# Transposing V and wq inside their own buffers in the backward part of a decode block

## The chip, the cores and the metric

The kernel runs on one core of one Trainium2 chip. The metric is device time in microseconds (us), the median over executions; the profile's span is one execution without its launch edges. A ratio is the mean time of one kernel's fast runs over that of the other's fast runs of the same rounds on the same chip, so it is not quite the ratio of the medians beside it.

## The reference

The reference is a pre-LayerNorm decode block and its gradients: attention of 4 x 32 heads over a cache of 4096 rows of 128, then a SwiGLU layer. It returns the output and the gradients of x, K, V and all weights. What matters for the change is the backward part of a head. With P the softmax row, dO the gradient of the head's output and c their constant:

```python
dV[k, :] = P[k] * dO                      # 1 MB per head, written
dP[k]    = V[k, :] . dO                   # needs V again, contracted over its 128 columns
dS[k]    = P[k] * (dP[k] - c) * scale
dK[k, :] = dS[k] * q                      # 1 MB per head, written
dx       = dq @ wq.T                      # needs wq transposed
```

K and V are read in the forward part, V is read a second time in the backward part, and dK and dV are written: 5 x 128 MB, nearly all of the traffic.

## The kernel before

Large tiles live in 23 slots of 8320 bytes per partition, handed out from a first-in first-out list `free`. A slot taken again waits for whatever its last user still does, for a gradient until its write has landed.

```python
class Slot:
    def __init__(self, name, src=free):
        self.i = src.popleft()
        self.t = slotp.tile([P, SLOT], BF16, name=name, tag=f"slot{self.i}")
    ...
    def give(self):
        free.append(self.i)
```

In the backward part V comes into 6 slots of a ring of its own (`vring`), is transposed on TensorE in blocks of 8 through PSUM, and ScalarE copies the blocks to a second slot, VT. That frees V's slot; VT is freed after the dP matmuls.

```python
def V_T(s, ps, part=range(SJ // GW)):
    if s not in VTs:
        VTs[s] = Slot("VT")
    VT, Vn = VTs[s].heads(), V2s[s].heads()
    for g in part:
        pt = ps.tile([P, GW, P], BF16, tag="tps", name="pt_tps")      # 2 PSUM buffers in the loop
        for i in range(GW):
            nc.tensor.transpose(pt[:, i, :], Vn[:, g * GW + i, :], ident_b[:])
        nc.scalar.copy(out=VT[:, g * GW:(g + 1) * GW, :], in_=pt[:])
    ...
    sl = V2s.pop(s)
    (vring if len(V2s) + len(vring) < NV2 else free).append(sl.i)

def front(s):
    ...
    for j in range(SJ):
        nc.tensor.matmul(dP_ps[:, j:j + 1], lhsT=VT[:, j, :], rhs=dOT_bf[:, s:s + 1], start=True, stop=True)
    VTs.pop(s).give()

for s in range(NH):                       # cut: the side work of the weight gradients
    prefetch()                            # loads V into every slot in vring
    front(s + 1); grad_V(s + 1); grad_K(s)
```

`grad_V` and `grad_K` each take a slot, fill it with one VectorE product, and have POOL issue its write to HBM.

## Time and profile before

| | before |
|---|---|
| median time of the first 3 runs | 1725.89 us |
| bytes moved | 707.88 MB |
| DMA share from 740 to 1700 us | 1.01 |
| busiest engine, PE | 77% of the span |

The prediction below shows the lines on the DMA. The other side of the picture is who waits for whom from 740 to 1700 us, the backward loop. The columns are the waiting engine, its line, what it waited for, us in total, times, longest.

```profile
POOL out_dram L780 <- DVE dSt L1162: 248.6, 86, 10.4
...
DVE gv L769 <- DMA out_dram<-gk: 128.5, 36, 11.7
PE pt_tps L759 <- ACT VT L760: 123.8, 131, 10.0
...
POOL out_dram L1169 <- DMA out_dram<-gk: 64.0, 21, 5.0
...
ACT VT L760 <- DMA out_dram<-gk: 53.8, 16, 8.5
```

The last line is what the change is aimed at. ScalarE (ACT) wants to copy a transposed block to VT, but the slot it was handed is still being written out as a K gradient. PE then waits for ScalarE (third line), and POOL for VectorE, which waits for dP (first line). The second line is a wait of the same kind by VectorE for its own output slot.

### The profile page before, as it was taken

The page shows a single profiled execution, that of the slowest core. Times are in us where ns is not written, and L with a number is a line of the kernel's source. Part 1 is how long each engine was busy: PE and PEld are TensorE (multiplying, and loading weights), DVE is VectorE, ACT ScalarE, POOL GpSimd, SP SyncE. Part 2 cuts the span into 40 slices and gives each one's busy share as a digit, 9 for nine tenths or more (in the row PEclk, how much of TensorE's full clock was granted, in tenths as well). Part 3 has the DMA queues.
Part 4 walks back from the last instruction along what each step waited for, and adds up shares of the span by engine and source line. Part 5 has one row for each costly group of instructions (what it writes and reads, how often), then busy time and mean ns, then how long its engine had stood idle before and what let it go on. Part 6 is the DMA issues. An engine that isn't in the chain of part 4 may idle for free.

```text
span 1721.7 us, 44266 instructions
## 1 busy us (share of the span) xinstructions
PE 1330.3 (77%) x19124; PEld 1129.6 (66%) x19124; DVE 1253.5 (73%) x1389; ACT 960.7 (56%) x1470; POOL 422.6 (25%) x808
## 2 busy tenths in 40 slices
PE   5889888888888888877688787786778677877672
PEld 4677666676666666867577677675666555656562
DVE  5989899989998997666766666665575566556573
ACT  3455444544444444667555555555666667766662
POOL 1211232222222231211322222221122223122231
PEclk9999999999999999666655555555675566555555
DMA  9999999999999999999999999999999999999997
GB/s 398 418 419 418 419 418 419 418 413 419 417 417 405 419 403 390 373 419 420 418 415 411 416 410 410 412 417 419 423 417 413 419 417 414 418 416 414 414 417 314
DMA packets 101868, 707.88 MB, mean 411 GB/s; under 512 B 11284, under 2 KB 15392, under 8 KB 17704
## 3 DMA queue, kind: packets, MB, share of 16 engines
q1 hardware_dynamic: 62272, 422.60, 59.5%
q0 software_dynamic: 39008, 282.37, 40.1%
q8 instruction: 150, 2.46, 0.5%
q14 instruction: 46, 0.38, 0.1%
q10 hardware_dynamic: 392, 0.07, 0.0%
HBM read 422.59 MB, written 282.34 MB: 409 GB/s over the span
## 4 chain that ended last, share of the span: by engine, by line
DMA 47%; DVE 6%; PE 4%; issue 3%; ACT 2%; POOL 0%; POOLq 0%; DVEq 0%; ACTq 0%
DMA out_dram<-gk 29%; DMA out_dram<-gv 14%; DVE gk L769 3%; DVE gv L769 2%; DMA out_dram<-gwq 2%; DMA out_dram<-gw 2%; ACT VT L760 1%; PE pt_tps L759 1%; PE M_ps L433 1%; DVE PK L418 1%; PE pt_w L562 0%; PE pt_wo L571 0%; ACT Pn L397 0%; POOL P L1143 0%; PE kP_ps L443 0%
## 5 line engine op out<-in xcount | busy, mean ns | idle before, releaser
L760 ACT COPY VT<-pt_tps 128x1024 bf16<-128x1024 bf16 x512 | 493.0, 1016 | 248.7 <-PE pt_tps L759 140.5
L759 PE MATMUL pt_tps<-ident_b,V 128*128 128x128 bf16 x4096 | 455.2, 293 | 129.6 <-ACT VT L760 125.2
L759 PEld LDWEIGHTS <-V 128*128 128x128 bf16 x4096 | 403.6, 138 | 193.3 <-issue 182.9
L769 DVE TENSOR_TENSOR gv<-P,reps 128x4096 bf16<-128x4096 bf16 x125 | 286.5, 2292 | 233.9 <-DMA out_dram<-gk 131.2
L769 DVE TENSOR_TENSOR gk<-dS,reps 128x4096 bf16<-128x4096 bf16 x128 | 293.4, 2292 | 99.7 <-DMA out_dram<-gv 55.8
L433 PE MATMUL M_ps<-PK,Vn 128*128 128x130 bf16 x4096 | 284.6, 222 | 49.0 <-DMA Vn<-in_A_v_cache_dram 48.6
L418 DVE TENSOR_TENSOR PK<-Kn,PK 128x4096 bf16<-128x4096 bf16 x128 | 292.3, 2283 | 31.6 <-POOL PK L414 31.2
L433 PEld LDWEIGHTS <-Vn 128*128 128x128 bf16 x4096 | 251.4, 99 | 70.3 <-DMA Vn<-in_A_v_cache_dram 64.2
L325 DVE STREAM_TRANSPOSE KT<-Kn 128x512 f32<-128x512 f32 (+1 forms) x321 | 250.6, 797 | 0.3 <-issue 0.2
L320 ACT COPY KT<-pt_tps 128x1024 bf16<-128x1024 bf16 x128 | 129.4, 1012 | 191.5 <-PE pt_tps L319 148.8
L1153 PE MATMUL dP_ps<-dOT_bf,VT 128*128 128x1 bf16 x4096 | 152.5, 166 | 66.3 <-ACT VT L760 65.0
L1153 PEld LDWEIGHTS <-VT 128*128 128x128 bf16 x4096 | 141.1, 104 | 78.5 <-ACT VT L760 77.4
L1169 POOL DMA_DIRECT2D out_dram<-gk x128 | 68.0, 531 | 374.0 <-DVE gk L769 250.4
L780 POOL DMA_DIRECT2D out_dram<-gv x128 | 68.2, 533 | 328.9 <-DVE dSt L1162 258.8
L331 POOL TENSOR_TENSOR W<-qrep,wmask 128x128 bf16<-128x128 bf16 x128 | 123.2, 963 | 83.4 <-PE S_ps L351 68.5
L414 POOL COPY PK<-P_all 128x64 bf16<-128x64 bf16 x128 | 32.4, 253 | 420.9 <-ACT P_all L408 417.9
L1143 POOL COPY P<-P_all 128x64 bf16<-128x64 bf16 x125 | 103.6, 829 | 0.0
L408 ACT COPY P_all<-pt_P 32x64 bf16<-32x64 bf16 x256 | 51.9, 203 | 58.9 <-PE pt_P L404 56.7
L319 PE MATMUL pt_tps<-ident_b,Kn 128*128 128x128 bf16 x1024 | 80.5, 223 | 0.0
L443 PE MATMUL kP_ps<-PK,onesw 128*32 128x512 bf16 x1024 | 79.6, 388 | 0.0
L319 PEld LDWEIGHTS <-Kn 128*128 128x128 bf16 x1024 | 62.0, 100 | 25.9 <-issue 25.8
L397 ACT ACTIVATE Pn<-E,rl 128x1024 bf16<-128x1024 f32 x64 | 73.7, 1152 | 3.3 <-DVE rl L394 3.2
(237 smaller groups left out, 1315.3 us busy)
## 6 DMA issues: line engine op xcount, KB each, us to landing
Kn<-in_A_k_cache_dram SPq DMA_DIRECT2D x128, 1024.0 KB, 15.4
Vn<-in_A_v_cache_dram SPq DMA_DIRECT2D x128, 1024.0 KB, 16.0
V<-in_A_v_cache_dram SPq DMA_DIRECT2D x128, 1024.0 KB, 10.7
out_dram<-gv POOLq DMA_DIRECT2D x128, 1024.0 KB, 24.8
out_dram<-gk POOLq DMA_DIRECT2D x128, 1024.0 KB, 25.3
wq<-in_A_wq_dram SPq DMA_DIRECT2D x8, 1024.0 KB, 13.2
out_dram<-gw POOLq DMA_DIRECT2D x6, 896.0 KB, 26.8
wo<-in_A_wo_dram SPq DMA_DIRECT2D x4, 1024.0 KB, 13.3
```

The lines of the kernel that those rows point to most:

```text
L319: nc.tensor.transpose(pt[:, i, :], Kn[:, c * GW + i, :], ident_b[:])
L320: nc.scalar.copy(out=KT[:, c * GW:(c + 1) * GW, :], in_=pt[:])
L325: nc.vector.transpose(out=KT[:, c * w_:(c + n) * w_], in_=Kn[:, c * w_:(c + n) * w_])
L331: nc.gpsimd.tensor_tensor(out=W[:, hl], in0=qrep[:, :, s:s + 1].to_broadcast([P, 4, 32]), in1=wmask[:, hl, None, :].to_broadcast([P, 4, 32 ...
L418: nc.vector.tensor_tensor(out=PK[:, :, 0:Dh].rearrange("p j (r t) -> p j r t", t=2), in0=Ks[s].heads().rearrange("p j (r t) -> p j r t", t=2),
L433: nc.tensor.matmul(hold["M"][:], lhsT=Vn[:, j, :], rhs=PK[:, j, :], start=(j == 0), stop=(j == SJ - 1))
L443: nc.tensor.matmul(hold["kP"][32 * q:32 * (q + 1), :, :], lhsT=ones_window(w), rhs=PK[:, j0:j0 + 4, 0:Dh], start=(w == 0 and c == 0), stop ...
L759: nc.tensor.transpose(pt[:, i, :], Vn[:, g * GW + i, :], ident_b[:])
L760: nc.scalar.copy(out=VT[:, g * GW:(g + 1) * GW, :], in_=pt[:])
L769: nc.vector.tensor_tensor(out=dst.rearrange("p j (r t) -> p j r t", t=2), in0=col2[:, :, None, :].to_broadcast([P, SJ, Dh // 2, 2]), in1=r ...
L1143: nc.gpsimd.tensor_copy(out=P2s[s][:], in_=P_all[:, s, :, None].to_broadcast([P, SJ, 2]))
L1153: nc.tensor.matmul(dP_ps[:, j:j + 1], lhsT=VT[:, j, :], rhs=dOT_bf[:, s:s + 1], start=True, stop=True)
```

## The change

The transposes write back into the block that they came from, so VT needs no slot. V's ring grows from 6 to 7 slots, and one more V is read ahead before the loop starts. wq in the dx stage is treated in the same way. The arithmetic and the order of the instructions stay, except for these slots and one V load.

```diff
     def V_T(s, ps, part=range(SJ // GW)):
         if s not in VTs:
-            VTs[s] = Slot("VT")
-        VT, Vn = VTs[s].heads(), V2s[s].heads()
+            VTs[s] = V2s.pop(s)
+        v = VTs[s].heads()
         for g in part:
 ...
-                nc.tensor.transpose(pt[:, i, :], Vn[:, g * GW + i, :], ident_b[:])
-            nc.scalar.copy(out=VT[:, g * GW:(g + 1) * GW, :], in_=pt[:])
-        if part[-1] < SJ // GW - 1:
-            return
-        sl = V2s.pop(s)
-        (vring if len(V2s) + len(vring) < NV2 else free).append(sl.i)
+                nc.tensor.transpose(pt[:, i, :], v[:, g * GW + i, :], ident_b[:])
+            nc.scalar.copy(out=v[:, g * GW:(g + 1) * GW, :], in_=pt[:])
 ...
-    NV2 = 6
+    NV2 = 7
 ...
-        while len(free) > 2:
+        while len(free) > 1:
             load_V2()
 ...
-            wqT = Slot("wqT")
 ...
-                    nc.scalar.copy(out=wqTv[:, h0:h0 + 8, :], in_=pt[:])
-                wq2.give()
+                    nc.scalar.copy(out=wv[:, h0:h0 + 8, :], in_=pt[:])
 ...
-            VTs.pop(s).give()
+            sl = VTs.pop(s)
+            (vring if len(V2s) + len(VTs) + len(vring) < NV2 else free).append(sl.i)
 ...
-                    V_T(1, psT)
                     first_gv[0].give()
```

More of the change, by code (lines that the diff above doesn't have):

```diff
@@ L985, in side_work @@
                 yield
-            wqTv = wqT.b(HD).rearrange("p (n c) -> p n c", c=P)
             for cc in range(DC):
@@ L992, in side_work @@
                 wq2 = wq2s.popleft()
+                wv = wq2.b(HD).rearrange("p (n c) -> p n c", c=P)
                 for h0 in range(0, H, 8):
@@ L995, in side_work @@
                     for i in range(8):
-                        nc.tensor.transpose(pt[:, i, :], wq2.b(HD)[:, (h0 + i) * P:(h0 + i + 1) * P], ident_b[:])
+                        nc.tensor.transpose(pt[:, i, :], wv[:, h0 + i, :], ident_b[:])
                     yield
-                    nc.scalar.copy(out=wqTv[:, h0:h0 + 8, :], in_=pt[:])
-                wq2.give()
+                    nc.scalar.copy(out=wv[:, h0:h0 + 8, :], in_=pt[:])
                 yield
                 for h in range(H):
-                    nc.tensor.matmul(dx_ps[0:B, cc * P:(cc + 1) * P], lhsT=dqT_bf[:, h * B:(h + 1) * B], rhs=wqTv[:, h, :],
+                    nc.tensor.matmul(dx_ps[0:B, cc * P:(cc + 1) * P], lhsT=dqT_bf[:, h * B:(h + 1) * B], rhs=wv[:, h, :],
                                      start=(h == 0), stop=(h == H - 1))
@@ L1005, in side_work @@
                         yield
+                wq2.give()
                 yield
-            wqT.give()
             yield
```

## The prediction

> **What bounds the kernel now.** I read the page from the top. The busiest engine is PE with 77% of the span, and the chain that ended last is mostly DMA, so I went to the row of slices and then to the transfers.
>
> ```profile
> PE 1330.3 (77%) x19124; PEld 1129.6 (66%) x19124; DVE 1253.5 (73%) x1389; ACT 960.7 (56%) x1470; POOL 422.6 (25%) x808
> ...
> DMA  9999999999999999999999999999999999999997
> ...
> DMA packets 101868, 707.88 MB, mean 411 GB/s; under 512 B 11284, under 2 KB 15392, under 8 KB 17704
> ...
> DMA 47%; DVE 6%; PE 4%; issue 3%; ACT 2%; POOL 0%; POOLq 0%; DVEq 0%; ACTq 0%
> ```
>
> No compute engine is near full, while the 16 DMA engines are at 9 in every slice but the last. The kernel must read K and V, read V again for the backward part, and write the gradients of both. That is 707.88 MB, and the change touches none of it. Full forward slices move 418 to 419 GB/s; at 419 the bytes alone need 707.88 / 0.419 = 1689 us. The span is 1721.7 us, so at most some 32 us (1.9%) is to be had by anything that leaves the bytes alone. To see where these 32 us lie I asked for busy time by stage (stretch, its length, five engines, granted clock, DMA share, GB/s):
>
> ```profile
> 0.00:20.00 20.00, 7.26 (x165) 6.47 (x166) 6.40 (x24) 2.46 (x4) 3.84 (x21) 1.00 0.92 372
> 20.00:660.00 640.00, 537.25 (x8884) 440.04 (x8884) 581.33 (x774) 318.61 (x702) 162.29 (x376) 0.99 1.01 416
> 660.00:700.00 40.00, 36.83 (x627) 30.00 (x624) 22.73 (x44) 19.95 (x38) 2.52 (x4) 0.96 1.03 388
> 700.00:740.00 40.00, 33.06 (x520) 30.16 (x516) 27.97 (x33) 27.41 (x31) 12.42 (x20) 0.66 0.94 369
> 740.00:1700.00 960.00, 715.86 (x8939) 622.89 (x8939) 615.06 (x517) 592.29 (x698) 241.49 (x387) 0.58 1.01 416
> 1700.00:1722.00 22.00, 0.00 (x0) 0.00 (x0) 0.00 (x0) 0.00 (x0) 0.00 (x0) 0.50 0.49 206
> ```
>
> Losses against 419 GB/s, as time: start 20 x (1 - 372/419) = 2.2 us; forward 640 x 3/419 = 4.6; the turn from forward to backward 40 x 31/419 + 40 x 50/419 = 3.0 + 4.8; backward 960 x 3/419 = 6.9; drain after the last issue 22 x (1 - 206/419) = 11.2. Their sum is 32.7, the gap to the bound. Only where the share is under 1 do transfers lack work; a share of 1.01 at 416 means busy engines with slower packets. Among the stages that the change touches, work is lacking only at the turn, and slices of 5 us put it here:
>
> ```profile
> 705.00:710.00 5.00, 4.12 (x92) 3.67 (x90) 4.85 (x5) 2.92 (x5) 0.63 (x1) 0.84 0.64 261
> 710.00:715.00 5.00, 4.41 (x56) 4.13 (x56) 4.58 (x5) 3.54 (x4) 4.71 (x5) 0.50 0.94 383
> 715.00:720.00 5.00, 4.39 (x63) 4.17 (x64) 4.61 (x5) 3.47 (x5) 2.17 (x4) 0.57 0.91 372
> ```
>
> That is 5 x (0.36 + 0.06 + 0.09) = 2.6 us of idle DMA. Between the V load issued at 701.3 us and the next at 719.6 us nothing is read, and the first gradient write is issued only at 707.7.
>
> **What the Trainium skill says.** "DMA: Bandwidth & Descriptors", section "Where 436 GB/s comes from", gives 435 GB/s as the fabric's ceiling and some 358 as a core's share of HBM. The trace sustains 416 to 419, so the share does not bind here with one core running, and little is left to the ceiling. The same page, "Issuing engines are not separate DMA queues", says that transfers run on the same 16 engines whichever engine issued them; the trace agrees: reads issued by SP and writes issued by POOL together make 416 in the backward part, so a read that comes sooner only displaces a write. Its section "Anatomy of one DMA" puts a transfer at 2.0 us + bytes / 436 GB/s, 4.4 us for 1 MB (an estimate by that page); the fastest gradient write took 5.3 us to land, the median 24.8 to 25.3, so some 20 us of a landing is queueing. Lastly "Perfetto Trace Analysis", section "Optimization Strategy", says repeated bubbles on the engine that should be saturated can mean too few buffers. There are none on the DMA after 720 us, though the compute engines show many.
>
> **The change part by part.** Work is not changed: 4096 transposes of V (293 ns), 512 copies by ScalarE (1016 ns), 4096 dP matmuls, 256 products by VectorE (2292 ns) and all transfers stay. Only waits and slots move.
>
> (a) The transposed head no longer takes a slot. In the 740 to 1700 us stretch ScalarE's copies waited for a gradient write to leave their slot: 53.8 us on gk, 26.7 on gv, 10.6 on gwq and 8.3 on gwo, together 99.4 us. These waits go. ScalarE has slack (592 of 960 us busy), so they matter only by delaying dP, dS and the next gradient. That delay costs time only if the DMA runs dry, and its share there is 1.01. Worth: 0.
>
> (b) Slots. Following the two programs' allocations in order, the loop of before begins with 5 slots shared in rotation by VT, gv and gk, and has 12 when half the heads are nearly done. Three takes per head bring a slot round after 5/3 heads, 12.6 us at (3 x 1.0486 MB) / 0.415 GB/ms = 7.58 us per head. Afterwards it is 4 slots and two takes: 2 heads, 15.2 us, and later 11 slots for 5.5 heads. Writes get more room, but they are held back elsewhere too: in the built programs the wait in front of a gradient write rotates over 8 semaphores, so write n waits for write n-8. At two per head that is 4 heads, 30 us, which the median landing of 25 us plus issue nearly fills. I expect VectorE's waits for slots (128.5 + 33.9 + 55.8 + 34.1 us) to move partly to POOL's waits for older writes (64.0 + 38.1 + 34.6 + 8 us). Worth: 0.
>
> (c) V's ring has 7 slots in place of 6, but a slot is free after the dP matmuls, not after the transposes: 1.5 to 2 us later by the timeline (two copies and the last 8 matmuls). One more V is read ahead. Loads land in 10.7 us against a lead of 6 heads, 45 us; transposes waited for V 2.3 us in all. Worth in the loop: 0.
>
> (d) At the turn the condition that leaves 1 slot free, not 2, issues V8 directly behind V7 at 701.3 us. That puts 1.0486 MB / 419 GB/s = 2.5 us of reading just ahead of the 2.6 us hole. What is read there is not read later: -2.0 to -2.5 us, the one gain that I can place.
>
> (e) wq in place: 16 copies and 128 transposes, the same as before, in a stage with ten or more free slots. The slot is held through 32 dx matmuls that the side work spaces over heads. Worth: 0.
>
> (f) The drain, 11 us, depends on how unevenly the last writes end on the 16 engines. The change does not address it; its scatter I guess at 2 us either way.
>
> Sum: 1725.9 - 2.3 = 1723.6; I say 1723.5.
>
> **The rivals.** First, in-place writing could serialize PE and ScalarE: if block g+1's transposes had to wait for block g's copy into the same tile, a head would cost 4 x (8 transposes at half clock, 1.03, + copy 1.02) = 8.2 us against 7.58, some +80 us. For it: the chain between 710 and 760 us alternates between exactly these two. Against it: in both built programs 264 of the 4096 V transposes carry a wait on ScalarE and 180 on PE, so dependencies follow blocks, and the two PSUM buffers still set the pace. I give it 1%.
>
> Second, only 4 output slots early in the loop could starve the writes: at 740 to 800 us a write landed in 9.6 to 14 us, and 2.3 for the product plus about 1.5 for issue gives 13.4 to 17.8 against 15.2 available. If writes wait and the ring of V is full, DMA goes idle: 6 heads by 1 us, +6 us at most, until the forward weights give slots back. Against it, before had a smaller share left for writes and still stayed at 1.01.
>
> Third, earlier gradients could change the mix or depth of traffic and with it the packet rate. The same loop shows 408 to 424 GB/s in 20 us slices. If the whole loop went to 419, it would be 6.9 us faster; at 413, 7 slower. Nothing shows a direction.
>
> Fourth, the removed waits could truly have bound the time, as the chain's 29% gk and 14% gv suggest. Then up to 99 us would go. But the byte bound allows only 32, of which 11 lie in the drain and 5 in the forward part.
>
> **Range and chances.** The third rival sets the width, the second and the drain add to it: 1715 to 1730 in 8 of 10. Faster by 2% would need under 1691.4 us, all but 2 us of the bound, drain and forward included: 0.5%. Slower by 2% needs 1760.4 us, and only the first rival reaches it: 1.5%.
>
> **What would show it.** The page after should still read 9 in every DMA slice, 707.9 MB, and 414 to 418 GB/s in the loop. ScalarE's V copies should show no wait for gradient writes; POOL should wait longer for writes and VectorE less. Two V loads should go out near 701 us, and the share in 705 to 710 us should rise from 0.64 to over 0.9. A share under 0.98 between 740 and 800 us would prove the second rival, a loop faster or slower than 960 us by over 8 us at share 1.01 the third. A span under 1710 us would mean that I misread what the slots cost.

## The result, and the profile after

The changed kernel takes 1723.03 us (median of 6 runs, 1721.68 to 1726.40) against 1726.18 us for the kernel before (6 runs). The ratio is 0.9982, with a 95% interval of 0.9964 to 0.9999: about 3 us faster, which counts as the same at 2%. On a second chip job it was 0.9976 (0.9963 to 0.9989).

The page of the changed kernel answers the page of before. The row of DMA slices still reads 9 in all but the last slice, and the chain is still made of writes:

```profile
DMA  9999999999999999999999999999999999999997
...
DMA packets 101867, 707.87 MB, mean 412 GB/s; under 512 B 11284, under 2 KB 15392, under 8 KB 17704
...
DMA out_dram<-gk 33%; DMA out_dram<-gv 15%; DMA out_dram<-gw 2%; ACT V L761 2%; DVE gk L766 1%; DVE gv L766 1%; PE pt_tps L760 1%; PE M_ps L433 1%; DVE PK L418 1%; PE pt_w L562 0%; PE gps L942 0%; ACT Pn L397 0%; PE kP_ps L443 0%; PE dP_ps L1148 0%; PE gu_ps L833 0%
```

The stages of the changed kernel, in the same columns as in the prediction:

```profile
700.00:740.00 40.00, 32.74 (x523) 29.66 (x520) 29.15 (x33) 27.27 (x31) 12.43 (x20) 0.66 0.95 378
740.00:1700.00 960.00, 712.74 (x8939) 616.53 (x8939) 615.80 (x516) 591.30 (x698) 268.38 (x387) 0.60 1.01 416
1700.00:1720.00 20.00, 0.00 (x0) 0.00 (x0) 0.00 (x0) 0.00 (x0) 0.00 (x0) 0.50 0.46 192
```

The loop moves 416 GB/s at a share of 1.01, just as before. The turn from 700 to 740 us moves 378 GB/s in place of 369, which is 40 us x 9 GB/s = 0.36 MB or 0.9 us at 419. The drain loses 20 x (1 - 192/419) = 10.8 us against 11.2. Slices of 5 us show what became of the hole at the turn:

```profile
700.00:705.00 5.00, 4.70 (x97) 4.26 (x95) 1.64 (x9) 2.25 (x3) 0.80 (x4) 0.76 0.96 374
705.00:710.00 5.00, 4.20 (x93) 3.82 (x91) 4.83 (x6) 2.91 (x5) 0.63 (x1) 0.84 0.92 382
710.00:715.00 5.00, 4.41 (x56) 4.13 (x56) 2.89 (x5) 3.45 (x4) 3.82 (x5) 0.50 0.96 392
715.00:720.00 5.00, 4.25 (x56) 4.03 (x57) 4.51 (x4) 3.43 (x5) 0.53 (x1) 0.53 0.78 321
```

From 705 to 710 us the share rose from 0.64 to 0.92, since two V loads now go out at 701.4 and 701.8 us. But from 715 to 720 us it fell from 0.91 to 0.78. The timeline of VectorE shows what came in between (start, duration, engine, line, operation, idle time before it and what ended it):

```profile
715.36 2.29 DVE L766 TENSOR_TENSOR gv<-reps 128x4096 bf16<-128x4096 bf16 x1 [2.24 <-DMA out_dram<-gv]
```

This product takes the slot of the very first V gradient, and now waits 2.24 us for that gradient's write; in the kernel before it had waited 0.18 us. The first write is issued at 707.7 us before and at 707.8 us in the changed kernel, where one more V read is in the DMA queues ahead of it. Counted from the packets of the traces, from 709 to 712 us the writes move 0.71 MB in place of 1.14, and the reads 0.47 in place of 0.06. So part of the hole was only moved.

The waits of the changed kernel in the loop, in the columns used above:

```profile
POOL out_dram L1165 <- DMA out_dram<-gk: 153.6, 47, 6.9
...
POOL out_dram L777 <- DVE dSt L1158: 72.1, 33, 4.1
...
PE dP_ps L1148 <- DVE dSt L1158: 60.5, 36, 6.7
...
PE pt_tps L760 <- ACT V L761: 51.9, 136, 3.1
...
ACT V L761 <- DMA out_dram<-gv: 4.2, 1, 4.2
```

The waits that the change was made for are gone: ScalarE's V copies wait 4.2 us in all for gradient writes, against 99.4. (Its whole idle time ahead of these copies fell less, from 241 to 185 us: 53.3 us are new, put down to no releaser. Where I followed them, at 1306 and 1322 us, they end with PE's transposes.) PE waits 51.9 us for ScalarE's copies, against 123.8. In their place PE waits 60.5 us for VectorE to empty a dP buffer, against 0.5 us before: the front of the loop now runs ahead until it meets the next limit. POOL waits 153.6 + 106.5 + 90.3 + 43.1 = 393.5 us for older gradient writes, against 64.0 + 38.1 + 34.6 + 8.3 = 145.0. So some 250 us of waiting moved from upstream of the products to the last step ahead of the DMA, and the DMA was as full as before.

### The profile page after: what moved, and what is told of

Same layout as the page of the kernel before. It is cut to its first block, busy times and chain, and to the rows that moved or that the text cites. A ratio compares the mean times of both kernels' runs of the same rounds, so it can differ in the third digit from the quotient of the medians.

```text
span 1719.8 us, 44279 instructions
## 1 busy us (share of the span) xinstructions
PE 1328.0 (77%) x19124; PEld 1124.5 (65%) x19124; DVE 1255.4 (73%) x1389; ACT 960.1 (56%) x1470; POOL 450.7 (26%) x808
## 4 chain that ended last, share of the span: by engine, by line
DMA 50%; PE 4%; DVE 3%; ACT 2%; issue 2%; POOL 0%; POOLq 0%; DVEq 0%; ACTq 0%
DMA out_dram<-gk 33%; DMA out_dram<-gv 15%; DMA out_dram<-gw 2%; ACT V L761 2%; DVE gk L766 1%; DVE gv L766 1%; PE pt_tps L760 1%; PE M_ps L433 1%; DVE PK L418 1%; PE pt_w L562 0%; PE gps L942 0%; ACT Pn L397 0%; PE kP_ps L443 0%; PE dP_ps L1148 0%; PE gu_ps L833 0%
## 5 line engine op out<-in xcount | busy, mean ns | idle before, releaser
L761 ACT COPY V<-pt_tps 128x1024 bf16<-128x1024 bf16 x512 | 492.5, 1016 | 192.0 <-PE pt_tps L760 131.8
L760 PEld LDWEIGHTS <-V 128*128 128x128 bf16 x4096 | 401.7, 138 | 122.3 <-issue 114.4
L766 DVE TENSOR_TENSOR gv<-P,reps 128x4096 bf16<-128x4096 bf16 x125 | 286.6, 2293 | 203.8 <-DMA out_dram<-gk 76.1
L766 DVE TENSOR_TENSOR gk<-dS,reps 128x4096 bf16<-128x4096 bf16 x128 | 293.4, 2292 | 108.5 <-DMA out_dram<-gv 54.3
L1148 PE MATMUL dP_ps<-dOT_bf,V 128*128 128x1 bf16 x4096 | 145.4, 166 | 107.4 <-DVE dSt L1158 60.5
L1148 PEld LDWEIGHTS <-V 128*128 128x128 bf16 x4096 | 138.8, 104 | 122.4 <-issue 66.7
L1165 POOL DMA_DIRECT2D out_dram<-gk x128 | 68.2, 533 | 401.2 <-DMA out_dram<-gk 153.6
L777 POOL DMA_DIRECT2D out_dram<-gv x128 | 68.4, 534 | 268.2 <-DMA out_dram<-gv 90.3
L1138 POOL COPY P<-P_all 128x64 bf16<-128x64 bf16 x125 | 127.4, 1019 | 0.0
L351 PE MATMUL S_ps<-KT,W 128*32 128x256 bf16 x1536 | 75.2, 285 | 0.5 <-DVE KT L325 0.2
```

What stands on the lines that cost most here:

```text
L760: nc.tensor.transpose(pt[:, i, :], v[:, g * GW + i, :], ident_b[:])
L761: nc.scalar.copy(out=v[:, g * GW:(g + 1) * GW, :], in_=pt[:])
L766: nc.vector.tensor_tensor(out=dst.rearrange("p j (r t) -> p j r t", t=2), in0=col2[:, :, None, :].to_broadcast([P, SJ, Dh // 2, 2]), in1=r ...
L1138: nc.gpsimd.tensor_copy(out=P2s[s][:], in_=P_all[:, s, :, None].to_broadcast([P, SJ, 2]))
```

## The experiments

Twelve kernels ran. x8 and x10 give a wrong K gradient, and all others match the reference. The table gives the ratio to the kernel before, and that ratio as us of 1726. Each interval is 2 to 4 us either way, so a difference between two rows is uncertain by some 3 us.

| run | edit | ratio (95% interval) | us |
|---|---|---|---|
| x0 | the changed kernel again | 0.9976 (0.9963 to 0.9989) | -4.1 |
| x1 | no V8 ahead | 0.9992 (0.9977 to 1.0006) | -1.4 |
| x2 | no V7 and V8 ahead | 1.0000 (0.9985 to 1.0015) | 0 |
| x3 | ring of 6, no V8 ahead | 1.0008 (0.9991 to 1.0026) | +1.4 |
| x6 | ring of 8 | 0.9987 (0.9975 to 0.9999) | -2.2 |
| x7 | 6 slots fewer from head 62 | 1.0024 (1.0002 to 1.0046) | +4.1 |
| x12 | wq not in place | 0.9979 (0.9965 to 0.9993) | -3.6 |
| x8 | 16 of 128 dK writes left out | 0.9756 (0.9742 to 0.9771) | -42 |
| x10 | 96 of 128 dK writes left out | 0.9296 (0.9282 to 0.9310) | -122 |
| x11 | 1 extra copy per head | 1.0277 (1.0262 to 1.0293) | +48 |
| x4 | 2 extra copies per head | 1.1034 (1.1018 to 1.1051) | +178 |
| x5 | one PSUM buffer | 1.2038 (1.2020 to 1.2056) | +352 |

### What the turn is worth: x0, x1, x2, x3

The theory was that only the hole at the turn matters, and that it counts one for one. The rival: the DMA engine that finishes last had a backlog through the hole, so filling it changes nothing.

x0 has no edit.

> The changed kernel itself, again, on the chip that also runs the next three, so that small differences are read on one chip. Theory (the DMA queues bound the time, the change only adds one early V load): ratio to before 0.9985, within 0.997 to 1.000. Rival (the slots freed are worth something in the loop): below 0.997.

x1 leaves 2 slots free, as before, so V8 isn't read ahead:

```diff
-        while len(free) > 1:
+        while len(free) > 2:
```

> The changed kernel, but leaving 2 slots free before the loop, as the kernel before does: V8 is not read early. If the hole at the turn sets what the change gains, the DMA share between 705 and 710 us falls back from 0.92 to about 0.64 and the time rises by 1 to 2.5 us to that of before (ratio to before 1.000). If the hole costs nothing, because the DMA engine that finishes last was not idle in it, the share falls in the same way and the time stays (ratio 0.998).

The hole came back, and the V load that should fill it goes out only at 716.2 us. These are the slices of x1:

```profile
705.00:710.00 5.00, 4.48 (x96) 4.04 (x93) 4.78 (x5) 3.24 (x5) 0.63 (x1) 0.84 0.61 252
710.00:715.00 5.00, 4.17 (x53) 3.97 (x54) 4.82 (x6) 3.19 (x4) 4.41 (x3) 0.50 0.88 360
715.00:720.00 5.00, 4.22 (x59) 3.91 (x56) 3.32 (x4) 3.43 (x4) 2.56 (x6) 0.53 0.71 220
```

x2 goes one load further, with `> 3`.

> The changed kernel with 3 slots left free before the loop: neither V7 nor V8 is read early, so 2 x 2.5 us of reading are missing ahead of the hole. If idle DMA time at the turn adds to the end one for one, the time is 4 to 5 us over the changed kernel. If the last DMA engine to finish sets the end and has a backlog through the hole, the rise is under 2 us.

x3 is the in-place transposes alone, with `> 2` and

```diff
-    NV2 = 7
+    NV2 = 6
```

> In-place transposes alone: the changed kernel with V's ring back at 6 slots and 2 slots left free, so that one more slot goes to the gradients (5, none for a transposed head). DMA theory: no gain in the loop, ratio to before 0.998 to 1.000. If output slots bound the loop, this is the best of all: 0.99 or lower.

Against x0, x1 is 0.0016 x 1726 = 2.8 us slower, x2 4.1 us and x3 5.5 us. The runs of x0, x1 and x2 are of the same rounds and can be compared directly: x1 is 2.6 us slower (95%: -0.1 to 5.4), x2 4.2 us (1.3 to 7.0). So x2 refutes the rival that nothing changes, and x1 alone is at the edge of the noise. From 660 to 740 us the kernels moved 382 (x0), 372 (x1), 372 (x2) and 366 GB/s (x3). Relative to x0 that is 80 x 10/419 = 1.9 us of traffic missing in x1 and x2, and 3.1 us in x3. Less traffic at the turn goes with a later end, but "one for one" is not shown. The kernel before moved 379 GB/s in this stretch and yet took as long as x2. And counted from the packets of the traces, x1 is 2.3 us of traffic behind x0 at 740 us but only 0.8 us behind at 1700 us, so its later end can't be put down to the hole alone.

x3 has the widest hole, with nearly half of this slice idle:

```profile
715.00:720.00 5.00, 4.22 (x63) 3.97 (x61) 4.34 (x4) 3.48 (x4) 3.22 (x4) 0.50 0.55 221
```

Its V8 load goes out at 723.0 us, against 719.6 before. About half of this comes from its whole turn being late in this execution (first gradient write at 709.5 us against 707.7). The rest, 1.6 us, fits a slot of the ring coming free after the dP matmuls rather than after the transposes. So in this trace in-place transposing alone widens the hole, and no variant without the load ahead is clearly faster than the kernel before. The counter-test, the load ahead in the kernel before, could not be made: with VT in a slot of its own no slot is left for the first gradient, and the program doesn't build (its list of free slots is empty at the first V gradient).

### Fewer output slots: x6 and x7

x6 has `NV2 = 8`, so 3 slots for gradients when the loop starts.

> The changed kernel with 8 slots for V in place of 7, so 3 slots for gradients when the loop starts. If the DMA has enough other work, the time stays within 2 us and the DMA share stays at 1.00 or more from 740 to 800 us. If three output slots starve the writes (reuse after 1.5 heads, 11.4 us, against 13.4 to 17.8 us for a product, its issue and its landing), heads early in the loop take 2 to 6 us longer until the forward weights give slots back: 10 to 30 us slower, with a share under 0.98 in that stretch.

The hole from 715 to 720 us closes, as V9 can be read at 716.1 us, with a share of 1.03. But then, in x6:

```profile
740.00:800.00 60.00, 44.50 (x585) 39.68 (x583) 38.37 (x35) 38.12 (x43) 15.02 (x25) 0.56 1.00 393
```

The share is 1.00 and the rate only 393 GB/s, where x0 has 422 and the changed kernel 417. The engines are busy with slower packets: in slices of 10 us the mean 8 KB read packet took 343 to 389 ns here against 310 to 317 in the changed kernel. The median is 309 ns in both, so it is a minority of slow packets, of up to 1.7 us. The loss, 60 x 24/417 = 3.5 us, takes back more than the filled hole gave: x6 is 1.8 us slower than x0 in the same rounds (95%: 0.5 to 3.2). It is not the starving that the expectation described (10 to 30 us), and why the packets are slow stays open.

x7 takes six slots away in the second half:

```diff
         for s in range(NH):
+            if s == 62:
+                for _ in range(6):
+                    free.popleft()
             prefetch()
```

> The changed kernel with 6 of its free slots taken away for good from head 62 on, when some 14 are free; the side work of the second half lives with the rest. Theory (with half the heads done, the rule that write n waits for write n-8 and the DMA rate hold the gradients back, and spare slots are worth nothing): within 3 us of the changed kernel, DMA share 1.01 from 1200 to 1650 us, VectorE's waits for slots up and POOL's waits for older writes down. Rival (slots are what the loop lacks): over 10 us slower.

This missed: x7 is 4.1 us slower than before and 7 to 8 us slower than the changed kernel, between the two forecasts of under 3 and over 10. POOL's waits for older writes vanish from its list, so slots are the limit there, and from 1300 to 1400 us it moves 401 GB/s at a share of 0.99 against 416 at 1.01:

```profile
1300.00:1400.00 100.00, 66.97 (x744) 50.91 (x745) 53.73 (x45) 61.74 (x82) 21.10 (x38) 0.59 0.99 401
```

By the program's allocations, 4 to 8 slots are free at the start of heads 62 to 115, shared with the side work, and the writes just fail to keep the DMA full. So spare slots are worth nothing only above some number, and in this half the changed kernel, with 10 to 15, lies above it. The number alone doesn't decide: in heads 1 to 7 the changed kernel has only 4, and its DMA share from 740 to 800 us is 1.01. What the side work of the second half adds was not tested.

### The wq part: x12

```diff
+            wqT = Slot("wqT")
 ...
-                    nc.scalar.copy(out=wv[:, h0:h0 + 8, :], in_=pt[:])
+                    nc.scalar.copy(out=wqTv[:, h0:h0 + 8, :], in_=pt[:])
+                wq2.give()
```

> The changed kernel with the wq part undone: the transposed wq again in a slot of its own. The same 128 transposes and 16 copies, in a stage with some 11 free slots, where x7 has shown that six slots less cost about 5 us over the whole second half. Theory: no difference from the changed kernel, ratio to before 0.9965 to 0.9995. If the wq part carried a share of the gain, 1.000 or above.

The ratio is 0.9979 against 0.9976 and 0.9982 for the full change. The wq part carries nothing that can be seen.

### Is it the bytes? x8 and x10

x8 leaves out every eighth K gradient's write:

```diff
+            if s % 8 != 7:
-            nc.gpsimd.dma_start(out=rows_of(out_2[b, h]), in_=gk.heads())
+                nc.gpsimd.dma_start(out=rows_of(out_2[b, h]), in_=gk.heads())
```

> The changed kernel without the write of every eighth K gradient: 16 x 1.0486 MB less, the result wrong on purpose, all computing kept. DMA theory: 16.8 MB / 416 GB/s = 40 us faster than the changed kernel. If the chain through the compute engines or the slots bound it, clearly less than 40.

The median is 1683.06 us, 40.1 us under the changed kernel's 1723.2 (38 by the ratios, as x0 ran on another chip), which is what 16.8 MB at 416 GB/s are worth. At this size of step the bytes alone set the time. x10 goes on to see where that ends, with `if s % 4 == 0:`.

> The changed kernel writing only every fourth K gradient (result wrong on purpose, all computing kept): 96 x 1.0486 MB less, by the DMA rate alone 100.7 MB / 416 GB/s = 242 us faster. After the run with more copies I expect the chain PE-ScalarE-PE of a head to take over at about 6.7 us a head (8.75 us there, less the two extra copies of 1.016): (7.58 - 6.7) x 128 = 113 us faster, between 80 and 150, with a DMA share well under 1. If compute had the room that ScalarE's busy share of 60% suggests, 242 us.

The median is 1603.42 us, 120 us faster and not 242. The DMA is no longer full (x10, the loop's steady stretch):

```profile
740.00:1500.00 760.00, 618.38 (x7926) 536.24 (x7927) 536.10 (x453) 521.23 (x617) 226.00 (x260) 0.63 0.93 356
```

Its first K gradient starts at 710.9 us and its last at 1594.8 us, so a head takes 883.9 / 127 = 6.96 us when little is written. Hardly anything waits for the DMA there (VectorE's V products 7.5 us in all for older writes, from 740 to 1500 us). So this is the pace of the compute chain, just under the 7.58 us that the DMA needs for a head.

### How near is the compute chain? x11, x4, x5

x11 and x4 copy one or two of the four blocks of a head twice:

```diff
+            for _ in range(2 if g == 0 else 1):        # x11;  x4: g % 2 == 0
-            nc.scalar.copy(out=v[:, g * GW:(g + 1) * GW, :], in_=pt[:])
+                nc.scalar.copy(out=v[:, g * GW:(g + 1) * GW, :], in_=pt[:])
```

> The changed kernel with one of the four copies of each head done twice (128 more copies of 1.016 us). If a head's chain is 6.7 us and the DMA needs 7.58, the sum is 7.7: 10 to 60 us slower, DMA share about 0.98 in the loop. If the chain has more room, under 4 us; if copies simply add to the time, 130 us.

> The changed kernel with two of the four copies of each head done twice: 256 more copies of 1.016 us, 260 us more work for ScalarE, which is then about 850 of the 960 us of the loop busy. DMA theory: within 4 us of the changed kernel, DMA share still 1.01 in the loop. If ScalarE's part of a head were on the path, up to 260 us slower.

x4 was expected to cost nothing, with ScalarE at 850 of 960 us. It cost 180 us. x11 cost 50 us for 130 us of copies. The same stretch as above, first of the changed kernel, then of x11, then of x4:

```profile
740.00:1500.00 760.00, 575.26 (x7256) 502.37 (x7257) 489.18 (x414) 467.14 (x545) 216.72 (x303) 0.61 1.01 416
```

```profile
740.00:1500.00 760.00, 572.10 (x6804) 511.01 (x6803) 454.62 (x386) 522.61 (x584) 204.62 (x283) 0.52 0.98 391
```

```profile
740.00:1500.00 760.00, 522.03 (x6131) 469.96 (x6131) 413.83 (x352) 544.02 (x592) 184.43 (x254) 0.52 0.90 350
```

The fourth busy column is ScalarE: 61%, 69% and 72% of the stretch. It is never near full, and still the extra copies cost time, because of the order of PE's work in the timeline. PE runs the last dP matmuls of a head, then a piece of side work, then the next head's first transposes, and ScalarE has nothing to copy meanwhile (2.67 us in the changed kernel at 1115 us). Four copies, that gap and the waits between them make the 6.96 us. One extra copy of 1.016 us makes 7.98, 0.40 over the DMA's 7.58, and 0.40 x 128 = 51 us; measured 50. Two make 8.99 and 180 us; measured 180. That these totals fit so closely is luck. Counted like x10's, from the first K gradient to the last, a head takes 8.28 us in x11 and 9.29 in x4, 0.3 more than the sums (and 7.68 in the changed kernel, 0.1 more than 7.58; the 8.75 in x10's expectation is not what x4 shows). The granted clock is lower in these two, 0.52 against 0.63 in x10, and a transpose took 304 to 305 ns on the mean against 287, which may be the 0.3. What is shown is that the chain needs about 7 us and that a copy more per head takes it over the DMA's pace.

x5 gives the transposes one PSUM buffer, the serial order of the first rival:

```diff
-        psT = c2.enter_context(tc.tile_pool(name="psT2", bufs=2, ...))
+        psT = c2.enter_context(tc.tile_pool(name="psT2", bufs=1, ...))
```

> The changed kernel with one PSUM buffer in place of two for the V transposes, so that each block's transposes wait for the copy of the block before: the serial order that the first rival feared. By the estimate in the prediction a head then costs 4 x (1.03 + 1.02) = 8.2 us plus dP about 1, against 7.58: 80 to 200 us slower, with a DMA share well under 1 in the loop. If PE and ScalarE have more room than that, the time stays within 10 us.

It cost 353 us. One head in its timeline shows PE and ScalarE strictly taking turns:

```profile
1104.23 1.01 PE L760 MATMUL pt_tps<-ident_b,V 128*128 128x128 bf16 x8 [1.10 <-ACT V L761]
...
1105.28 1.01 ACT L761 COPY V<-pt_tps 128x1024 bf16<-128x1024 bf16 x1 [1.10 <-PE pt_tps L760]
1106.35 1.01 PE L760 MATMUL pt_tps<-ident_b,V 128*128 128x128 bf16 x8 [1.10 <-ACT V L761]
...
1108.70 1.42 PE L953 MATMUL dq_ps<-dOT_f,M 128*128 128x1 f32 x6
```

From its first K gradient at 712.6 us to its last at 2064.8 a head takes 10.65 us.

## Why the prediction was right or wrong

**The bound.** Right. All DMA slices stayed full, the bytes stayed, and x8 moved the time by just its bytes.

**(a) and (b), waits and slots.** The worth of zero held, and 99 us of ScalarE's waiting went without a gain. The destination was half wrong. The prediction wanted VectorE's waits for slots to move to POOL; they stayed (252.3 us before, 76.1 + 73.3 + 54.3 + 46.8 = 250.5 after). What POOL gained in waiting for older writes came instead with the loss of POOL's waits for VectorE: for dSt from 248.6 to 72.1 us and for gk from 242.9 to 94.0. x7 adds that slots do matter once six fewer are left.

**"ScalarE has slack (592 of 960 us busy)".** Misjudged, though the time didn't depend on it. The chain's own pace is 6.96 us against 7.58 (x10), a margin of 8% where the busy share suggests 38%.

**(c) the later release.** The size was right: 1.5 to 2 us were predicted, and x3's V8 load is 1.6 us later once the late start of its turn is taken off. In the loop it is worth nothing, as said. The prediction did not ask what it costs at the turn when the load ahead is missing; x3, 1.4 us slower than before with an interval that takes in zero, can't say either.

**(d) the load ahead.** This was the one gain placed, at 2.0 to 2.5 us. Taking it away cost 2.6 to 2.8 us (x1), with an uncertainty of about 3 us, so the gain is likely and its size is not confirmed. In the profile the hole was only partly filled, a net 0.9 us, since the read also delayed the first write, whose slot the fourth product needs. The prediction overlooked that. Its "nothing is read" is also too strong: no V load is issued from 701.3 to 719.6 us, but packets of the earlier reads run on until just under 710 us.

**(e) wq and (f) the drain.** Nothing, as said: x12, and 10.8 us against 11.2.

**The sum.** 1723.5 was predicted, 1723.03 measured. That they agree to 0.5 us is luck, as single executions of the changed kernel spread over nearly 5 us. The size of the gain was 2.3 us predicted and 3 to 4 measured, with 2 to 3 us of uncertainty. The two profiled executions differ by only 1.9 us in span. Of that, 0.9 us shows at the turn and 0.4 in the drain; the rest is below what these runs resolve, and I leave it open. One comparison in the prediction sets device time (1691.4) against span (1689), which is some 1.8 us shorter: a gain of 2% would have needed all but about 0.5 us of the bound, not all but 2. Nothing rests on this.

**The rivals.** The first did not occur, and its price was mis-sized: 8.2 us per head and +80 us in the prediction, 10.65 us and +353 measured in x5. The estimate left out the dP matmuls, the side work and the hand-overs between the engines. The second (4 slots starve the writes) is refuted by a share of 1.01 from 740 to 800 us. The third, a changed packet rate, may have shown itself in x6; in the changed kernel the loop kept 416 GB/s. The fourth is refuted: the waits went and the time stayed.

## What to carry to other kernels

When all slices of the DMA are full, count the bytes first: removing a wait upstream only lets the next one appear, here in front of the write queue. The place where a saved buffer can pay is a stage in which the saturated resource runs dry, so find that stage and use the buffer there. Do not read an engine's slack from its busy share when it works in turns with another; give it more work and see when the time moves.

## What the Trainium skill lacked or had wrong

- "Perfetto Trace Analysis", section "Identifying the Most-Contended Engine", calls the occupancy of ScalarE "also a fair measure of how close you are to roofline". As a measure of slack it misleads here: ScalarE was 62% busy in the loop, and one extra copy per head, 130 us in all, already cost 50 us (x11).
- "DMA: Bandwidth & Descriptors", section "Where 436 GB/s comes from", says that for transfers between HBM and SBUF the HBM side (some 358 GB/s) binds. That sentence doesn't hold with one core running, as the page's own single-core measurements above it also show: the loop sustained 416 GB/s of reads and writes together for 960 us.
- I found no page on how the 16 DMA engines end a long stream: after the last write is issued (1699.5 us before) the rate falls gradually, and the drain loses some 11 us in both kernels.
- I found no page that tells why packets get slower while all 16 engines are busy: in x6 the share is 1.00 from 740 to 800 us with 393 GB/s, and in the changed kernel 1.01 with 417.
